# Moving two groups of buffers in SBUF: the operands of two large products of an attention and softplus feed-forward kernel

## The chip, the cores and the metric

The kernel runs on one core of a Trainium2 chip. The metric is the device time of one execution in microseconds, here the median of three executions. TensorE (PE, with its weight loads shown apart as PEld), VectorE (DVE), ScalarE (ACT), GpSimd (POOL) and the DMA queue of SyncE (SP) work side by side and are tied by semaphores.

## What is computed

```python
# q, k, v: (8, 8, 576, 64); w_in: (512, 2048); w_out: (2048, 512); all float32
scores = scale * q_chunk @ k_chunk.T          # chunks of 64 positions
attn = exp(scores - max) / (sum + 1e-9)
x = (attn @ v_chunk) as (4608, 512)
h = x @ w_in
g = maximum(h, 0) + log1p(exp(-abs(h)))       # softplus
out = g @ w_out                               # (4608, 512)
```

## The kernel before

The 4608 rows of x are taken in nine groups (`m`) of 512, and the 2048 inner columns in sixteen chunks (`fc`) of 128. For each of these 144 blocks there is a first product (`gemm1`, matmuls at line 567), a softplus chain on ACT and DVE (`u` at line 578, `g_hi` at 582, `g_lo` at 586) and a second product (`gemm2`, matmuls at line 600). The order on PE is first product of block n, second product of block n - 1, first product of block n + 1, and so on. Between them stand short bursts of 64-wide matmuls (lines 449 and 530) that make the attention of later rows; lines 342 to 390 make the attention of the first rows.

Every float32 operand is split into a high and a low part (type fp32r, 4 bytes an element), and each product is the sum of three: low times high, high times low, high times high. A matmul loads one operand into PE (LDWEIGHTS, 128 columns, 512 bytes of each partition) and streams the other past it (512 columns, 2048 bytes of each partition).

- First product, a block has 12 matmuls: four slices `c` of 128 inner rows, three terms each. Loaded: a slice of the input weights (`wi_hi`, `wi_lo`, or `wib` for the second half of the chunks). Streamed: x, as eight runs of 64 elements (256 bytes) that stand 1024 bytes apart; slice `c` begins `c` times 256 bytes into the tile.
- Second product, a block has 12 matmuls: four tiles of 128 rows, three terms each. Loaded: 128 columns of `g_lo` or `g_hi`. Streamed: one row of output weights of 512 consecutive elements (`wo_hi`, `wo_lo`, `wo_end`, or a `late` buffer).

One load belongs to each matmul and runs while the matmul before it streams; so the last matmul of a first product streams x while the first `g_lo` is loaded, and the last of a second product streams output weights while the first `wi_lo` is loaded.

```python
# gemm1, line 567: out, loaded, streamed
nc.tensor.matmul(ph, wt[:, c, fs], x[:, ts_, c, :], ...)
# gemm2, line 600
nc.tensor.matmul(pos[w["m"]][t], gg[:, ts_], wt, ...)
```

The order of all engines comes from a planner (class `Plan`) with fixed costs; it is settled before the kernel runs and knows nothing of addresses. Addresses come from the tile pools: each pool is laid behind the one before (`later`, `late`, `const`, `xpool`, `ld`, `att`, `sp`), and inside a pool the tiles stand in the order in which they were first asked for, each rounded up to 32 bytes.

Of the kernel before, what the change touches and what calls it, by code (L numbers as in the profile page):

```python
# [11 lines left out]
F32 = mybir.dt.float32  # L12
F32R = mybir.dt.float32r
I32 = mybir.dt.int32
# [3 lines left out]
BF16 = mybir.dt.bfloat16  # L18
# [129 lines left out]
def chunked_attention_softplus_ffn(  # L148
# [12 lines left out]
    P = 128  # L161
# [14 lines left out]
    UW = 512  # L176
    RAW_BUFS = 3
# [2 lines left out]
    FILL = 0.8  # L180
    LATE = 15
    STAGED = 15

    later = ctx.enter_context(tc.tile_pool(name="later", bufs=2))
    late = ctx.enter_context(tc.tile_pool(name="late", bufs=LATE))
    const = ctx.enter_context(tc.tile_pool(name="const", bufs=1))
    xpool = ctx.enter_context(tc.tile_pool(name="xpool", bufs=4))
    ld = ctx.enter_context(tc.tile_pool(name="ld", bufs=1))
    att = ctx.enter_context(tc.tile_pool(name="att", bufs=1))
    sp = ctx.enter_context(tc.tile_pool(name="sp", bufs=2))  # L190
# [5 lines left out]
    ident = const.tile([P, P], F32, name="ident")  # L196
    make_identity(nc, ident)
    half = DF // 2
    wi = [tuple(const.tile([P, KC, half], F32R, name=n) for n in ("wi_hi", "wi_lo"))]
    stage = [later.tile([P, KC * half], F32, name="wib") for _ in range(2)]  # L200
    wo_hi = const.tile([P, HALF_FC, DM], F32R, name="wo_hi")
# [16 lines left out]
    tops = [const.tile([P, UW], I32, name=f"top{j}") for j in range(TOP_BUFS)]  # L218
    for t in tops:
        nc.vector.memset(t, 0)  # L220
    live = {}

    def raw_tile():
        return ld.tile([P, 2 * UW + 2], I32, name="raw", bufs=RAW_BUFS)

# [1 line left out]
    def w_load(u, is_in, fc):  # L229
        queue = nc.gpsimd if u in LOAD_POOL else nc.sync  # L230
        raw = raw_tile()
        st = raw.bitcast(U16)[:, 1 : 4 * UW + 1]
        if is_in:
            queue.dma_start(
                st.rearrange("p (c f) -> p c f", c=KC),
                w_in_v[:, :, 4 * fc * P : 4 * (fc + 1) * P],
            )
        else:
            queue.dma_start(st, w_out_v[:, fc, :])
        live["raw", u] = raw  # L240

    def w_top(u):
        live["top", u] = tops[0]
        tops.append(tops.pop(0))
        top = live["top", u].bitcast(F16).rearrange("p (f t) -> p f t", t=2)[:, :, 1]
        src = live["raw", u].bitcast(BF16)[:, 4:].rearrange("p (f t) -> p f t", t=4)[:, :, 0]
        (nc.gpsimd.tensor_copy if u not in TOP_ACT else nc.scalar.copy)(top, src)  # L247

    def w_low(u):
        if u < STAGED:  # L250
            o = u * UW
            low = stage[o // (KC * half)][:, o % (KC * half) :][:, :UW].bitcast(I32)
        else:
            low = ld.tile([P, UW], I32, name="low", bufs=LOW_BUFS)
        src = live.pop(("raw", u)).bitcast(U32)[:, 1 : 2 * UW + 1].rearrange("p (f t) -> p f t", t=2)[:, :, 0]
        nc.scalar.activation(low, src, AF.Copy, scale=2.0**-13)
        live["low", u] = low
# [347 lines left out]
    def evacuate(w, t):  # L605
        if t % 2 == 0:
            live["out", w["m"], t // 2] = raw_tile()
        o = live["out", w["m"], t // 2][:, t % 2 * DM : (t % 2 + 1) * DM].bitcast(F32)
        (nc.vector.tensor_copy if t % 2 else nc.scalar.copy)(o, pos[w["m"]][t])
        live["o", w["m"], t] = o  # L610
# [55 lines left out]
    for u, (g, is_in, fc) in enumerate(units):  # L666
        (of_in if is_in else of_out)[fc] = u
        d = due(g) - 4
        last = [f"w_hi{u}", f"w_lo{u}"]
        users = []  # L670
        if not is_in and fc >= HALF_FC:
            for j in range(2 * (fc - HALF_FC), min(2 * (fc - HALF_FC) + 2, LATE)):
                users.append("EVVSS"[j % 5] + str(j // 5))
        pl = "POOL" if u in LO_POOL else "DVE"
        ph_ = "POOL" if u in HI_POOL else "ACT"
        staged = u < STAGED
        pool = u in LOAD_POOL
        plan.add(f"load{u}", "POOL" if pool else "SP", 0.75 if pool else 0.55, partial(w_load, u, is_in, fc),
                 urg=d - LEAD if u else LQ, kb=480,
                 take=[("raw", [f"w_top{u}", f"w_low{u}"])], after=[LOAD_AFTER])  # L680
        on_act = u in TOP_ACT
        plan.add(f"w_top{u}", "ACT" if on_act else "POOL", 0.78 if on_act else 0.77, partial(w_top, u), [f"load{u}"],
                 urg=d, take=[("top", [f"w_add{u}"])])
        plan.add(f"w_low{u}", "ACT", 0.67, partial(w_low, u), [f"load{u}"], urg=d + 0.01,
                 take=[] if staged else [("low", last)], after=[f"w_top{u}"])
        plan.add(f"w_add{u}", "DVE", 0.68, partial(w_add, u), [f"w_top{u}", f"w_low{u}"], urg=d + 1.4, port=True)
        freed = []
        if is_in and fc == HALF_FC:
            freed = [f"w_{n}{j}" for n in ("hi", "lo") for j in range(STAGED)]
        if fc:  # L690
            freed.append(f"w_hi{(of_in if is_in else of_out)[fc - 1]}")
        plan.add(last[0], ph_, 0.63 if ph_ == "POOL" else 0.61, partial(w_hi, u, is_in, fc),
                 [f"w_add{u}"] + users + freed, urg=d + 2.1)
        plan.add(last[1], pl, 1.3 if pl == "POOL" else 0.65, partial(w_lo, u, is_in, fc, pl == "POOL"),
                 [last[0]] + users, urg=d + 2.8)
# [111 lines left out]
    for w in ahead + blocks:  # L807
        g, m, fc, name = w["g"], w["m"], w["fc"], w["name"]
# [58 lines left out]
```

## Time and profile before

| | |
|---|---|
| runs | 876.37, 878.07, 879.29 us; median 878.07 us |
| the profiled execution | 878.49 us |
| its span, first to last instruction | 876.7 us |
| PE busy | 861.6 us, 98% of the span |
| PE weight loads busy | 701.5 us, 80% |
| DVE, ACT, POOL busy | 348.5, 309.4, 65.3 us |
| 16 DMA engines, share of the span | 32% |

The profile gives for each group of instructions the line, the engine, the operation, the tile that is written and those that are read. The duration of a matmul is longer than its distance to the next, since matmuls are pipelined; the distance from one start to the next tells the pace. "Granted clock" 1.00 is 2.4 GHz, 0.5 is 1.2 GHz.

### The profile page before, as it was taken

The page shows a single profiled execution, that of the slowest core. Times are in us where ns is not written, and L with a number is a line of the kernel's source. Part 1 is how long each engine was busy: PE and PEld are TensorE (multiplying, and loading weights), DVE is VectorE, ACT ScalarE, POOL GpSimd, SP SyncE. Part 2 cuts the span into 40 slices and gives each one's busy share as a digit, 9 for nine tenths or more (in the row PEclk, how much of TensorE's full clock was granted, in tenths as well). Part 3 has the DMA queues.
Part 4 walks back from the last instruction along what each step waited for, and adds up shares of the span by engine and source line. Part 5 has one row for each costly group of instructions (what it writes and reads, how often), then busy time and mean ns, then how long its engine had stood idle before and what let it go on. Part 6 is the DMA issues. An engine that isn't in the chain of part 4 may idle for free.

```text
span 876.7 us, 14820 instructions
## 1 busy us (share of the span) xinstructions
PE 861.6 (98%) x5874; PEld 701.5 (80%) x5874; DVE 348.5 (40%) x589; ACT 309.4 (35%) x483; POOL 65.3 (7%) x68
## 2 busy tenths in 40 slices
PE   8799999999999999999999999999999999999998
PEld 7677888888888888888888888888888888888886
DVE  5999964333424161525242342334241614121111
ACT  4576744332423242424242332324232424222222
POOL 0564741000000000000000000000000000000000
PEclk9999999999999999999999999999999999999999
DMA  9787753322232224231322223122322241000001
GB/s 223 186 210 218 174 146 90 67 40 49 42 96 43 49 42 104 35 63 29 71 70 56 43 47 97 39 50 42 96 42 51 41 105 33 17 29 20 1 1 48
DMA packets 209958, 63.65 MB, mean 73 GB/s; under 512 B 187105, under 2 KB 203233, under 8 KB 209889
## 3 DMA queue, kind: packets, MB, share of 16 engines
q1 hardware_dynamic: 209888, 62.71, 31.9%
q8 instruction: 46, 0.75, 0.4%
q14 instruction: 24, 0.19, 0.1%
HBM read 45.09 MB, written 9.44 MB: 62 GB/s over the span
## 4 chain that ended last, share of the span: by engine, by line
PE 89%; DMA 4%; DVE 4%; SPq 1%; issue 1%; ACT 1%; POOL 0%; DVEq 0%; POOLq 0%; ACTq 0%
PE po L600 42%; PE pa L567 41%; PE pa L530 2%; DMA raw<-in_moe_w_in_dram 2%; PE pa L449 2%; DMA raw<-in_moe_w_out_dram 1%; PE po L330 1%; DVE wib L261 1%; SPq L322 1%; DVE mx L494 0%; DVE den L510 0%; DMA q<-in_q_dram 0%; DMA x<-in_v_dram 0%; DVE g_lo L586 0%; DVE x L546 0%
## 5 line engine op out<-in xcount | busy, mean ns | idle before, releaser
L578 ACT ACTIVATE u<-pa 128x512 f32<-128x512 f32 (+1 forms) x145 | 86.2, 594 | 510.1 <-PE pa L567 505.4
L586 DVE TENSOR_TENSOR g_lo<-u,g_hi 128x512 fp32r<-128x512 f32 (+1 forms) x137 | 94.9, 693 | 295.3 <-ACT g_hi L582 295.0
L567 PE MATMUL pa<-x,wib 128*128 128x512 f32 x864 | 208.6, 390 | 0.0
L567 PEld LDWEIGHTS pa<-x,wib 128*128 128x128 f32 x864 | 161.7, 188 | 36.0 <-PE po L600 2.4
L567 PE MATMUL pa<-x,wi_hi 128*128 128x512 f32 (+1 forms) x584 | 179.3, 389 | 2.1 <-DVE x L546 2.1
L600 PE MATMUL po<-late,g_hi 128*128 128x512 f32 x540 | 172.1, 394 | 0.0
L567 PEld LDWEIGHTS pa<-x,wi_hi 128*128 128x128 f32 x584 | 109.9, 189 | 24.3 <-DVE x L546 2.3
L600 PEld LDWEIGHTS po<-late,g_hi 128*128 128x128 f32 x540 | 101.2, 187 | 24.4
L567 PE MATMUL pa<-x,wi_lo 128*128 128x512 f32 (+1 forms) x292 | 114.0, 390 | 1.3 <-POOL top L247 1.0
L600 PE MATMUL po<-wo_hi,g_lo 128*128 128x512 f32 x288 | 114.9, 399 | 0.0
L600 PE MATMUL po<-late,g_lo 128*128 128x512 f32 x288 | 114.6, 398 | 0.0
L600 PE MATMUL po<-wo_lo,g_hi 128*128 128x512 f32 x288 | 114.0, 396 | 0.0
L600 PE MATMUL po<-wo_hi,g_hi 128*128 128x512 f32 x288 | 113.5, 394 | 0.0
L582 ACT CAST g_hi<-u 128x512 fp32r<-128x512 f32 (+1 forms) x145 | 89.4, 616 | 4.4
L567 PEld LDWEIGHTS pa<-x,wi_lo 128*128 128x128 f32 x292 | 55.2, 189 | 15.7 <-PE po L600 2.9
L600 PEld LDWEIGHTS po<-wo_hi,g_lo 128*128 128x128 f32 x288 | 54.3, 188 | 13.1
L600 PEld LDWEIGHTS po<-wo_hi,g_hi 128*128 128x128 f32 x288 | 54.1, 188 | 13.2
L600 PEld LDWEIGHTS po<-late,g_lo 128*128 128x128 f32 x288 | 54.0, 187 | 13.0
L600 PEld LDWEIGHTS po<-wo_lo,g_hi 128*128 128x128 f32 x288 | 54.1, 188 | 12.8
L494 DVE TENSOR_REDUCE mx<-pa 128x8 f32<-128x512 f32 x32 | 22.0, 686 | 69.4 <-ACT x L542 69.0
L426 DVE STREAM_TRANSPOSE qe<-q 128x512 f32<-128x512 f32 x29 | 20.5, 707 | 65.5 <-DMA k<-in_k_dram 46.3
L426 DVE STREAM_TRANSPOSE ka<-k 128x512 f32<-128x512 f32 x29 | 20.6, 711 | 51.1 <-DMA k<-in_k_dram 33.8
(101 smaller groups left out, 565.9 us busy)
## 6 DMA issues: line engine op xcount, KB each, us to landing
out_dram<-raw SPq DMA_DIRECT2D x36, 256.0 KB, 2.4
raw<-in_moe_w_in_dram SPq DMA_DIRECT2D x16, 512.0 KB, 5.0
raw<-in_moe_w_out_dram SPq DMA_DIRECT2D x16, 512.0 KB, 5.0
eT<-ka SPq DMA_DIRECT2D x248, 32.0 KB, 1.9
q<-in_q_dram SPq DMA_DIRECT2D x232, 32.0 KB, 2.2
k<-in_k_dram SPq DMA_DIRECT2D x232, 32.0 KB, 2.1
q<-in_v_dram SPq DMA_DIRECT2D x60, 64.0 KB, 2.5
k<-in_v_dram SPq DMA_DIRECT2D x60, 64.0 KB, 2.5
```

Of the source, the lines that this page charges most:

```text
L261: nc.vector.tensor_tensor(low, low, live.pop(("top", u)), op=ALU.add)
L322: nc.sync.dma_start(dv[a * C : (a + 1) * C, :, c2, :], v[b, a * HP : (a + 1) * HP, c * C : (c + 1) * C, :].rearrange("h s d -> s h d"),)
L330: nc.tensor.matmul(dst[:, :P], ident, ident, start=True, stop=True)
L426: nc.vector.transpose(t, live.pop((n, i)))
L449: nc.tensor.matmul(pa[o, c2, col : col + C], qT[r, a * HP + hl, :], kT[r, a * HP + hl, :], start=True, stop=True,)
L494: nc.vector.tensor_reduce(mx, sc, axis=AX.X, op=ALU.max)
L530: nc.tensor.matmul(pa[o, a, col : col + C], vt[r, 4 * j + 2 * h2 + c2, :], eT[r, :, 4 * c2 + 2 * j + h2, :], start=True, stop=True,)
L567: nc.tensor.matmul(ph, wt[:, c, fs], x[:, ts_, c, :], start=(n == 0), stop=(n == 3 * KC - 1))
L578: nc.scalar.activation(w["u"], w["ph"], AF.Softplus)
L582: nc.scalar.copy(w["hi"], w["u"])
L586: (nc.gpsimd if pool else nc.vector).tensor_tensor(w["lo"], w["u"], w["hi"].bitcast(F32), op=ALU.subtract)
L600: nc.tensor.matmul(pos[w["m"]][t], gg[:, ts_], wt, start=(w["first"] and n == 0), stop=(w["last"] and n == 2),)
```

## The change

```diff
+    G_PAD = 48
+    X_PAD = 64
...
     half = DF // 2
+    sp.tile([P, G_PAD], F32, name="pad", bufs=1)
     wi = [tuple(const.tile([P, KC, half], F32R, name=n) for n in ("wi_hi", "wi_lo"))]
...
     for t in tops:
         nc.vector.memset(t, 0)
+    const.tile([P, X_PAD], F32, name="x_pad")
     live = {}
 
     def raw_tile():
-        return ld.tile([P, 2 * UW + 2], I32, name="raw", bufs=RAW_BUFS)
+        return ld.tile([P, 2 * UW + 16], I32, name="raw", bufs=RAW_BUFS)
...
-        src = live["raw", u].bitcast(BF16)[:, 4:].rearrange("p (f t) -> p f t", t=4)[:, :, 0]
+        src = live["raw", u].bitcast(BF16)[:, 4 : 4 * UW + 4].rearrange("p (f t) -> p f t", t=4)[:, :, 0]
```

A pad of 256 bytes goes behind the constants, one of 192 bytes ahead of the softplus buffers, and each of the three `raw` buffers (weights as they arrive, and output on its way out) grows from 4104 to 4160 bytes. Nobody reads or writes the pads. The last edit takes the same elements of `raw` as before. Every engine's instructions, their order and their waits are the same before and after; only addresses differ. The pads move what lies behind them:

| buffers | begin at byte, by the remainder of 512: before | after |
|---|---|---|
| `wib`, `late`, `ident`, `wi_hi`, `wi_lo`, `wo_hi`, `wo_lo`, `wo_end`, `top` | 128 | 128 |
| `x` (also the early loads in its place) | 128 | 384 |
| `raw`, three of them | 128, 160, 192 | 384, 448, 0 |
| `q`, `k`, `low`, `eT`, `qe`, `ka` | 224 | 64 |
| `u`, `g_hi`, `g_lo` | 352 | 384 |

From the tile's start and the slice follows where the operands of the two products begin, by the same remainders:

| product | loaded, before and after | streamed, before | streamed, after |
|---|---|---|---|
| first, slices `c` = 0 and 2 | 128, 128 | 128 | 384 |
| first, slices `c` = 1 and 3 | 128, 128 | 384 | 128 |
| second, all 12 | 352, 384 | 128 | 128 |

## Rows read from the trace of the kernel before

**Rows 1.** The page: busy times, and the span in 40 slices.
```profile
PE 861.6 (98%) x5874; PEld 701.5 (80%) x5874; DVE 348.5 (40%) x589; ACT 309.4 (35%) x483; POOL 65.3 (7%) x68
...
PE   8799999999999999999999999999999999999998
...
PEclk9999999999999999999999999999999999999999
```

**Rows 2.** Waits of PE, longest first in total (us, times, longest).
```profile
PE pa L567 <- DVE x L546: 2.1, 1, 2.1
...
PE pa L530 <- DMA x<-in_v_dram: 1.2, 2, 0.6
```

**Rows 3.** Two stretches, instructions of line 600 alone (busy, count, granted clock, DMA).
```profile
0.00:126.00 126.00, 42.27 (x168) 31.79 (x168) 0.99 0.81 199
126.00:872.60 746.60, 385.14 (x1560) 291.25 (x1560) 1.00 0.24 50
```

**Rows 4.** The chain that ended last, its end (start us, us, what).
```profile
859.13 2.73 PE pa L567 x12
861.86 2.79 PE po L600 x12
864.65 2.73 PE pa L567 x12
867.38 5.61 PE po L600 x24
```

**Rows 5.** Timeline of PE, one first product and six blocks later (start us, us).
```profile
502.25 0.39 PE L600 MATMUL po<-late,g_hi 128*128 128x512 f32 x1
502.48 0.39 PE L567 MATMUL pa<-x,wi_lo 128*128 128x512 f32 x1
...
503.16 0.39 PE L567 MATMUL pa<-x,wi_lo 128*128 128x512 f32 x1
...
503.84 0.39 PE L567 MATMUL pa<-x,wi_lo 128*128 128x512 f32 x1
...
504.52 0.39 PE L567 MATMUL pa<-x,wi_lo 128*128 128x512 f32 x1
...
535.60 0.39 PE L567 MATMUL pa<-x,wi_lo 128*128 128x512 f32 x1
```

**Rows 6.** Line 600 from 499.6 to 502.47 us: duration ns min/median/max; then its last alone.
```profile
L600 PE MATMUL po<-late,g_hi x8: 389/394/397, 499.9 to 502.2; 128*128 128x512 f32 x8
L600 PE MATMUL po<-late,g_lo x4: 393/395/397, 499.7 to 501.8; 128*128 128x512 f32 x4
...
L600 PE MATMUL po<-late,g_hi x1: 389/389/389, 502.2 to 502.2; 128*128 128x512 f32 x1
```

**Rows 7.** The same of line 567 in 502.47 to 505.1 us; then its last alone.
```profile
L567 PE MATMUL pa<-x,wi_hi x8: 389/389/396, 502.7 to 505.0; 128*128 128x512 f32 x8
...
L567 PE MATMUL pa<-x,wi_hi x1: 396/396/396, 505.0 to 505.0; 128*128 128x512 f32 x1
```

**Rows 8.** Groups of PE by shape, 126 to 870 us (busy us, mean ns).
```profile
L567 PE MATMUL pa<-x,wib 128*128 128x512 f32 x768 | 185.5, 390 | 0.0
...
L600 PE MATMUL po<-late,g_lo 128*128 128x512 f32 x260 | 103.5, 398 | 0.0
...
L600 PE MATMUL po<-wo_hi,g_hi 128*128 128x512 f32 x256 | 100.7, 393 | 0.0
```

**Rows 9.** Timeline of PE: 64-wide matmuls of the first attention rows.
```profile
15.29 1.09 PE L364 MATMUL po<-late 64*64 64x64 f32 x30
...
20.61 1.09 PE L364 MATMUL po<-ka,qe 64*64 64x64 f32 x30
...
24.08 0.69 PE L390 MATMUL pa<-late 64*64 64x64 f32 x32 [0.68 <-ACT late L378]
...
29.68 0.69 PE L390 MATMUL pa<-x,eT 64*64 64x64 f32 x32 [0.60 <-ACT x L378]
```

**Rows 10.** The chain between 75 and 125 us, and waits of ACT after 126 us.
```profile
78.56 3.37 DMA x<-in_v_dram
...
118.44 3.99 DMA raw<-in_moe_w_out_dram
...
ACT u L578 <- PE pa L567: 493.5, 126, 5.4
```

## The prediction, made before the changed kernel was run

> **What bounds the kernel now.** I read the page first: PE is busy for 98% of the span and its clock is full in all but a sliver [rows 1], so the reader is to look for what sets the pace of PE's own instructions. The waits of PE come next: the longest single one is 2.1 us, in the first 126 us, and for DMA it waits 1.2 us in all [rows 2]. The chain at the end of the run is PE alone, product after product, down to the last output [rows 4]. ACT, the engine behind PE in the softplus chain, waits 493.5 us for PE after 126 us [rows 10]. So after the start nothing but the spacing of matmuls counts, and a nanosecond of a matmul is a nanosecond of the run.
>
> Now the spacing. The first product takes its slices at 502.48, 503.16, 503.84 and 504.52 us [rows 5]: three matmuls in 0.68 us, 226.7 ns each. The second product is slower. Six whole blocks take 535.60 - 502.48 = 33.12 us [rows 5], 5.520 us a block; 24 matmuls at 226.7 ns would be 5.440 us. There are 80 ns over in each block, and a block has twelve loads of g: **6.7 ns for each load of g**. The end of the run, where two second products follow each other, agrees: 5.61 us for 24 matmuls is 233.8 ns each, 7.1 ns more than 226.7 [rows 4].
>
> Is it the load of g, or the streaming of output weights, that costs this? The last matmul of each product tells, since it streams one kind and loads the other. The last of a second product streams output weights while an input weight is loaded: 389 ns, like the matmuls of the first product, where its eleven neighbours have 393 to 397 [rows 6]. The last of a first product streams x while g is loaded: 396 ns, where its neighbours have 389 [rows 7]. So the price goes with the load of g, whatever is streamed. The groups over the whole run say the same, 390 ns against 393 to 398 [rows 8]. What sets a load of g apart from one of an input weight, in the table of remainders, is that it begins at 352 and not at 128.
>
> **The change part by part.** No instruction, wait or transfer is added or taken away; only addresses move.
>
> *x from 128 to 384.* Slices 0 and 2 streamed from 128 and will stream from 384; slices 1 and 3 go the other way. Half of the first product is 256 bytes apart before, and the other half after. And it costs the same either way: slice 0 (no distance) takes 0.68 us, slice 1 (256 apart) 0.68 us, slice 2 again 0.68 us [rows 5]. This part is worth nothing, in either direction.
>
> *g from 352 to 384.* The distance to the streamed operand goes from 224 to 256, and the load's own start from a remainder of 352 to one of 384. The trace has no load of 128 columns at 384. The ends: at best the load costs nothing at all and a matmul takes its 512 columns at the granted 2.4 GHz, 213.3 ns (20 ns less than now); at worst it costs as much as or more than it does at 352. The nearest row is the load at 128 beneath the very same streamed output weights, at 389 ns and so at the pace of 226.7 ns [rows 6], and 384 differs from 128 by just the 256 bytes that made no difference with x. I take 226.7 ns.
>
> The sum: 1560 matmuls of line 600 start after 126 us [rows 3], with as many loads of g, and PE waits for nobody there: 1560 x 6.7 ns = 10.4 us. The 168 before that [rows 3] could give 1.1 us, but there PE also waits, and the chain runs through transfers of v and of weights [rows 10]; those come no sooner, so I count half, 0.5 us. Together 10.9 us.
>
> *The other buffers.* `ka`, `qe`, `eT`, `q` and `k` go from 224 to 64. Both operands of the 64-wide matmuls are among them. Thirty such matmuls from `late` (128) take 1.09 us and thirty from `ka` and `qe` (224) take 1.09 us; thirty-two at line 390 take 0.69 us with `late` and 0.69 us with `eT` [rows 9]. So the bursts gain and lose nothing. DVE and ACT work on moved buffers too; what they take is covered by ACT's 493.5 us of waiting for PE [rows 10], and would show only if a chain of softplus fell behind by microseconds in each block. Transfers land at other remainders: no row tells remainders apart; I count nothing, and as ends the 1.2 us that PE waits for DMA now [rows 2], gained or doubled.
>
> 878.49 us of the profiled execution less 10.9 is 867.6 us. That execution was 0.4 us over the median of the runs, so for the median I say **867.2 us**.
>
> **The rivals.**
>
> *No change.* The price of a load of g may come from what the pads leave alone: g was written by ACT and DVE shortly before, and it lies near the end of the memory. For it: every load of g has these too, and the 64-wide loads from 224, as odd a start as 352, are no slower than those from 128 [rows 9]. Against it: those same 64-wide loads come from buffers high in memory, filled shortly before, and are not slow either; and all twelve loads of a block cost about the same, early or late in the product [rows 6]. It gives 878.1 us. [...]
>
> *The whole stall goes.* If 256 bytes is the distance at which loading does not disturb streaming, the second product would fall to 213.3 ns: 20 ns x 1560 = 31.2 us, 847 us. Against it: half of the first product stands at that distance and pays its 226.7 ns like the rest [rows 5]. What is left for it is that x is streamed in runs of 256 bytes and output weights in one of 2048. [...]
>
> *Half the price.* A load at 384 may pay part of what one at 352 pays, say 3.3 ns: 5.2 us gained, 873 us. No row has such a middle value.
>
> *Slower.* The price may grow with the distance by remainders between load and stream: nothing at 0, 6.7 ns at 224, and more at 256. In proportion it would be 7.6 ns: 0.9 ns x 1560 = 1.5 us more, 879.6 us. It shows as slower from 1.7 ns a load on (2.6 us, 880.7 us). Against it: the last matmul of a first product streams x from 384 with g loaded from 352, 32 bytes apart, and pays as much [rows 7]; and x at a distance of 256 pays nothing more [rows 5].
>
> **How the numbers follow.** A measurement of this kernel can tell about 0.3%, 2.6 us. Chances: the price of g goes and the rest stays, 78%; no change 10%; the whole stall 5%; half the price 4%; slower 3%. Faster 0.87, same 0.10, slower 0.03. Within the likeliest case the smallest gain is 1560 loads at the 5 ns that the groups of rows 8 differ by, 7.8 us (870.3 us), and the largest all 1728 at 7.1 ns, 12.3 us (865.8 us); with what transfers may do, the range is 864.5 to 870.5 us.
>
> **What would show it.** Right: six blocks in about 32.6 us; first and second product both at 226.7 ns; 389 ns for every matmul of both lines, the last of a first product too; line 567 unchanged in slices 0 and 1; bursts as before. Wrong: matmuls of line 600 still at 393 to 398 ns (no change), well under 389 (the whole stall), or over 398 (slower); or a spacing that falls while PE begins to wait for DMA or for g after 126 us.

## The result, and the profile after

The changed kernel takes 868.13 us (median of four, 867.25 to 870.22) against 877.35 us of the kernel before on the same chip (four runs): a ratio of 0.9896, 95% interval 0.9869 to 0.9922. That is 9.2 us less (6.8 to 11.5 us by the interval); 10.9 us were forecast, to 867.2 us, and 868.1 us lies in the range. The profiled execution took 867.25 us, with a span of 865.5 us.

The chain at the end of the changed kernel (start us, us, what; line 604 is the former 600, line 571 the former 567):

```profile
848.16 2.72 PE pa L571 x12
850.88 2.72 PE po L604 x12
853.60 2.72 PE pa L571 x12
856.32 5.45 PE po L604 x24
```

These answer to [rows 4]. The second product took 2.79 us and takes 2.72 us, as long as the first; the closing run of 24 fell from 5.61 to 5.45 us, 227 ns a matmul.

The timeline of PE at the seam of the two products, as in [rows 5]:

```profile
495.99 0.39 PE L571 MATMUL pa<-x,wi_lo 128*128 128x512 f32 x1
...
496.67 0.39 PE L571 MATMUL pa<-x,wi_lo 128*128 128x512 f32 x1
...
497.35 0.39 PE L571 MATMUL pa<-x,wi_lo 128*128 128x512 f32 x1
...
498.03 0.39 PE L571 MATMUL pa<-x,wi_lo 128*128 128x512 f32 x1
...
498.71 0.39 PE L604 MATMUL po<-late,g_lo 128*128 128x512 f32 x1
...
528.63 0.39 PE L571 MATMUL pa<-x,wi_lo 128*128 128x512 f32 x1
```

Slice after slice takes 0.68 us, as before, though each has changed places: slice 0 now streams from 384 and slice 1 from 128. Six blocks take 528.63 - 495.99 = 32.64 us, as forecast (33.12 us before). The second product's durations, ten of its twelve matmuls at line 604 between 492 and 495.5 us (ns min/median/max), against 389/394/397 of [rows 6]; then all twelve of the first product that begins at 495.99 us, whose last one took 396 ns before [rows 7]:

```profile
L604 PE MATMUL po<-late,g_hi x6: 389/389/389, 493.5 to 495.1; 128*128 128x512 f32 x6
L604 PE MATMUL po<-late,g_lo x4: 389/389/389, 493.3 to 495.3; 128*128 128x512 f32 x4
...
L571 PE MATMUL pa<-x,wi_hi x8: 389/389/389, 496.2 to 498.5; 128*128 128x512 f32 x8
L571 PE MATMUL pa<-x,wi_lo x4: 389/389/389, 496.0 to 498.0; 128*128 128x512 f32 x4
```

Where nothing is saved: the blocks that hold a burst. First the kernel before, then the changed one, at the same block (timeline; the DVE row is the one that empties the burst's PSUM tile, the PE row the next first product):

```profile
258.49 0.69 PE L530 MATMUL pa<-eT,q 64*64 64x64 f32 x32
...
262.77 0.68 DVE L499 TENSOR_TENSOR qe<-pa,mx 128x512 f32<-128x512 f32 x1
...
263.59 0.47 PE L567 MATMUL pa<-x,wi_lo 128*128 128x512 f32 x1
```

```profile
254.84 0.69 PE L534 MATMUL pa<-eT,q 64*64 64x64 f32 x32
...
259.12 0.68 DVE L503 TENSOR_TENSOR qe<-pa,mx 128x512 f32<-128x512 f32 x1
...
259.94 0.47 PE L571 MATMUL pa<-x,wi_lo 128*128 128x512 f32 x1
```

From the start of the burst to the next first product it is 5.10 us in both, though a second product stands between them; in twelve of the fifteen bursts after 120 us it is 5.10 to 5.11 us in both kernels. DVE ends at 263.45 and at 259.80 us, and the first product starts 0.14 us later each time: there DVE sets the start, and what the second product gains is waited out ahead of the next first product. The waits of PE after 126 us list none of this: the ends of matmuls are modelled, and the last matmul ahead of the gap, which starts at 263.20 us before, is given 0.40 us and so fills it.

### The profile page after: what moved, and what is told of

Same layout as the page of the kernel before. It is cut to its first block, busy times and chain, and to the rows that moved or that the text cites. A ratio compares the mean times of both kernels' runs of the same rounds, so it can differ in the third digit from the quotient of the medians.

```text
span 865.5 us, 14820 instructions
## 1 busy us (share of the span) xinstructions
PE 850.3 (98%) x5874; PEld 701.7 (81%) x5874; DVE 345.5 (40%) x589; ACT 309.3 (36%) x483; POOL 66.1 (8%) x68
## 4 chain that ended last, share of the span: by engine, by line
PE 89%; DVE 4%; DMA 2%; issue 1%; ACT 1%; POOL 1%; SPq 1%; DVEq 0%; POOLq 0%; ACTq 0%
PE po L604 42%; PE pa L571 42%; PE pa L534 2%; PE pa L453 2%; DMA raw<-in_moe_w_out_dram 1%; SPq L326 1%; PE po L334 1%; DMA raw<-in_moe_w_in_dram 1%; DVE den L514 1%; DVE wib L265 0%; POOL top L251 0%; DVE eT L477 0%; DVE g_lo L590 0%; DVE low L265 0%; ACT u L582 0%
## 5 line engine op out<-in xcount | busy, mean ns | idle before, releaser
L604 PE MATMUL po<-late,g_hi 128*128 128x512 f32 x540 | 169.3, 389 | 0.0
L604 PEld LDWEIGHTS po<-wo_hi,g_hi 128*128 128x128 f32 x288 | 54.3, 189 | 11.5
L604 PEld LDWEIGHTS po<-late,g_lo 128*128 128x128 f32 x288 | 54.0, 188 | 11.5
```

The costliest lines, as they stand in the source:

```text
L604: nc.tensor.matmul(pos[w["m"]][t], gg[:, ts_], wt, start=(w["first"] and n == 0), stop=(w["last"] and n == 2),)
```

## The experiments

All moves below are made with pads alone, so the instructions and their order are those of the kernel before. "Distance" is where the load starts less where the stream starts.

**Which of the moves it is.** The first runs moved u, g_hi and g_lo alone:

```diff
     half = DF // 2
+    sp.tile([P, 8], F32, name="pad", bufs=1)      # g at 384; 72: at 128; 40: at 0; 120: at 320
```

> The kernel before with u, g_hi and g_lo alone moved from 352 to 384; x, raw and all else stay. Theory A (a load pays by its own start: free at a multiple of 64 bytes, 6.7 ns elsewhere) and theory B (a load pays by its distance from the streamed operand's start, by remainders of 512: nothing at 0 and 256, 6.7 ns at 224): both expect the whole gain of the change, line 600 at 389 ns and 226.7 ns from start to start, about 868 us. If the moves of x, raw or q and k gave part of it, it stays short of that: 870 us or more.

Measured: 867.75 us against 877.43 us, ratio 0.9895 (0.9871 to 0.9919). The chain's rows read as in the changed kernel:

```profile
856.87 2.72 PE pa L568 x12
859.59 5.45 PE po L601 x24
```

So 32 bytes ahead of g give the whole gain. The counterpart moved x and left g:

```diff
+    sp.tile([P, 64], F32, name="pad", bufs=1)
...
+    const.tile([P, 64], F32, name="x_pad")
```

> x alone moved from 128 to 384; g stays at 352 (raw goes to 384, 416 and 448, q, k and their like to 480 on the way). If x matters as the change's words have it, line 567 and the last matmul of a first product get another price. By the equal slices of the trace before: no change, 877 us, line 567 at 389 ns, line 600 at 393 to 397 ns as before. One thing may shift: the first load of g of a block now runs beneath x streamed from 128, not 384.

Measured: 877.9 us against 879.05 us, ratio 0.9987 (0.9972 to 1.0002).

```profile
865.95 2.73 PE pa L569 x12
868.67 5.61 PE po L602 x24
```

To the hundredth these are the rows of before [rows 4]: x gives nothing.

**Is 256 bytes of distance needed?**

> The kernel before with u, g_hi and g_lo alone moved to 128, so that g is loaded from the same remainder from which output weights stream (distance 0). Theory A: free, 389 ns, about 868 us. What the change's words suggest (loaded and streamed operand must begin 256 bytes apart): the price stays or grows, 393 ns and more, 877 us or more. Theory B as read from input weights loaded under output weights (distance 0 at no price): about 868 us.

Measured: 868.03 us, ratio 0.9895 (0.9876 to 0.9915).

```profile
852.15 2.72 PE pa L568 x12
854.87 5.45 PE po L601 x24
```

No: with loaded and streamed operand at the same remainder it is as fast.

**The load's own start, or the distance?**

> The kernel before with u, g_hi and g_lo alone moved to 0, so the distance to the streamed operand is 384 (or 128 the other way) and each load of 512 bytes begins on a multiple of 512. Theory A: free, 389 ns, about 868 us. Theory B (in proportion to the nearer distance, 128): 3.8 ns a load, about 872 us. A third: the 13.3 ns that every matmul has over 512 columns at 2.4 GHz come from loads that begin at 128 or 384 and never at a multiple of 512; then line 600 falls below 226.7 ns, the run below 865 us.

Measured: 881.57 us, ratio 1.0045 (1.0030 to 1.0061): 0.45% slower than before, little, but clear of the noise.

```profile
868.70 2.76 PE pa L568 x12
871.46 5.60 PE po L601 x24
```

> The kernel before with u, g_hi and g_lo alone moved to 320: a multiple of 64 and not of 128, at a distance of 192. Theory A: free, 389 ns, about 868 us. Theory A with a grain of 128 bytes: the price stays, 393 to 398 ns, about 877 us. Theory B: 5.7 ns a load, about 876 us.

Measured: 872.51 us, ratio 0.9941 (0.9922 to 0.9959), in the middle.

```profile
858.68 2.72 PE pa L568 x12
861.40 5.51 PE po L601 x24
```

Theory A falls with these two: 0 and 320 are multiples of 64, and both pay. In proportion to the nearer distance, theory B fails too (0 costs more than it said, 320 less). To part distance from place, everything was then moved under an unmoved g:

```diff
+    later.tile([P, 120], F32, name="first_pad", bufs=1)     # all that stood at 128 to 96
...
+    sp.tile([P, 8], F32, name="pad", bufs=1)                # g back at 352
```

> Everything that stood at 128 moved to 96 (wib, late, wi, wo, x and the rest), g left at 352, its dear place: both products now have distances of 0 and 256 as in the changed kernel, but no load begins where it was free so far. Theory D (distance): all matmuls at 389 ns, 226.7 ns apart, about 868 us. Theory O (own start): loads of g stay dear (877 us), and loads of input weights at 96 may become so too (885 us and more).

Measured: 869.34 us against 879.05 us, ratio 0.9898 (0.9872 to 0.9925).

```profile
855.82 2.72 PE pa L569 x12
858.54 5.45 PE po L602 x24
```

g is loaded from 352, where it cost 6.7 ns in the kernel before, and costs nothing, because the streams now start at 96. **The distance decides, not the load's own start.**

> The kernel before with g alone moved to 256, a distance of 128 from the streamed output weights, the mirror of g at 0. Theory D with a price that depends on the distance taken either way round: like g at 0, about 5.5 ns a load and some more in the first product, about 881 us. If the direction counts (load ahead of or behind the stream), something else. Theory O: starts on multiples of 256 are dear: about 881 us too.

Measured: 881.81 us against 879.05 us, ratio 1.0029 (1.0016 to 1.0041).

```profile
868.13 2.76 PE pa L568 x12
870.89 5.60 PE po L601 x24
```

The rows are those of g at 0: distances of 128 and of 384 cost the same, and the medians from one start to the next agree at each of the 24 places of a block to 1 ns. With 0 and 256 alike free, what counts is the distance by remainders of **256**. By 256 the two are one distance, so this run says nothing on a mirror.

> The changed kernel with wi_hi and wi_lo at 160 and wo_hi, wo_lo and wo_end at 192; wib and late stay at 128, x and g at 384. So in the first eight chunks the loads of the first product begin at 160 (x streams from 384 or 128: distance 224 or 32) and those of the second at 384 with streams from 192 (distance 192). Theory D (the distance decides: free at 0 and 256, about 2.5 ns at 192, 6.7 ns at 224): matmuls with wi_hi and wi_lo pay about 4 to 7 ns, those with wo_hi and wo_lo about 2.5 ns, those with wib and late nothing: 72 blocks x 12 x (5 + 2.5) ns = 6.5 us, about 874.5 us. Theory O (the load's own start decides: free at 128 and 384): wi_hi and wi_lo pay, wo_hi and wo_lo do not: about 872 us.

```diff
+    const.tile([P, 8], F32, name="wi_pad")        # wi_hi, wi_lo: 128 to 160
...
+    const.tile([P, 8], F32, name="wo_pad")        # wo_hi, wo_lo, wo_end: 128 to 192
...
-    X_PAD = 64
+    X_PAD = 48
```

Measured: 876.8 us against 879.05 us, ratio 0.9977 (0.9966 to 0.9988); by the two ratios some 7 us of the changed kernel's gain are lost, near what theory D says. With the intervals it could be 4 to 10 us, so the time alone hardly tells theory O (some 4 us) from theory D. The chain does, since by theory O the second product would pay nothing. The chain, first in chunks with `wi_hi`, `wi_lo` and `wo_hi`, `wo_lo`, then in chunks with `wib` and `late`:

```profile
324.43 2.80 PE pa L573 x12
327.23 2.75 PE po L606 x12
...
855.75 2.72 PE pa L573 x12
858.48 2.72 PE po L606 x12
```

The first product, never dear before, pays 2.80 us as soon as its own load stands 32 from its stream (160 under 128, or under 384, which is the same by 256). The second pays 2.75 us with g at 384 and streams from 192, as it did with g at 320 and streams from 128: the same distance of 192, the same price, another place. So it has nothing to do with g being fresh, or high in memory.

**The other distances** (g alone again, `sp` pads of 88, 96 and 112 elements; one run each).

> g alone at 192: distance 64 from the streamed output weights. If the price repeats every 256 bytes of distance and is the same either way round (ahead or behind), it is that of 192: 2.5 ns a load, line 600 of before at 388 to 394 ns. If it grows from 32 (6.7 ns) to 128 it lies above 6.7 ns. If it repeats every 64 bytes it is that of 128: 5.5 ns and a slower start of the first product.

```profile
866.37 2.75 PE pa L568 x12
869.12 5.61 PE po L601 x24
```

> g alone at 224: distance 96. If the price is that of 32 wherever the distance is an odd multiple of 32, 6.7 ns; if it is the mirror of 160, the same as the run with g at 288.

```profile
865.76 2.73 PE pa L568 x12
868.50 5.63 PE po L601 x24
```

> g alone at 288: distance 160, the mirror of 96. The same price as g at 224 if only the size of the distance counts; 6.7 ns if every odd multiple of 32 costs that.

```profile
869.46 2.77 PE pa L568 x12
872.23 5.61 PE po L601 x24
```

With g at 192, 224 and 288 the single times are 880.24, 879.66 and 883.35 us, against 878.63 us. All expectations of a mirror or of a fixed price for odd multiples of 32 miss. A distance of 64 comes out near that of 128, but a price that repeats every 64 bytes is excluded by 0 and by the cheap 192. A block without a burst, first plus second product, in one trace for each distance (the sum of their median times from start to start, after 126 us):

| distance by 256 | 0 | 64 | 96 | 128 | 160 | 192 | 224 |
|---|---|---|---|---|---|---|---|
| block, us | 5.44 | 5.55 | 5.54 | 5.55 | 5.57 | 5.47 | 5.52 |

(32 was measured in the first product alone: 2.80 us against 2.72.) Only 0 is free. The side counts: 192 is cheap, 64 is not. And the price does not end with the loads that cause it: with g at 0 the first product, its operands untouched, takes 2.76 us. From start to start its first seven matmuls take 224 to 236 ns, the next four 227 ns, as in the kernel before. Its durations between 868.5 and 871.3 us there, where the kernel before has 389 for all but the last [rows 7]:

```profile
L568 PE MATMUL pa<-x,wib x12: 387/391/397, 868.5 to 871.1; 128*128 128x512 f32 x12
```


**What is left above the stream.** In the kernel before the granted clock is 0.50 from 34.9 to 38.2 us (timeline of PE in that stretch):

```profile
35.14 0.41 PE L567 MATMUL pa<-x,wi_lo 128*128 128x256 f32 x1
...
37.06 0.63 PE L600 MATMUL po<-wo_hi,g_lo 128*128 128x512 f32 x1
37.49 0.63 PE L600 MATMUL po<-wo_lo,g_hi 128*128 128x512 f32 x1
```

Nine matmuls of 256 columns take 37.06 - 35.14 = 1.92 us there, 213.3 ns each, and the first of 512 columns takes 0.43 us to the next: 1.2 columns a nanosecond at a clock of 0.50. At 1.00 that makes an estimated 2.4 a nanosecond and 213.3 ns for 512 columns; in the traces, this is what the 2.4 GHz and the 213.3 ns of the prediction rest on. The measured 226.7 ns are 13.3 ns more than this estimate.

```diff
+                rows = C if n == 1 else P
                 nc.tensor.matmul(
-                    pos[w["m"]][t], gg[:, ts_], wt,
+                    pos[w["m"]][t][:rows], gg[:, ts_][:, :rows], wt,
```

> The changed kernel, but the middle term of each tile in the second product (g_hi times the low weights) loads 64 columns in place of 128 and makes 64 output rows of its 128; the other 64 rows lack that term. Every matmul of the two products is 226.7 ns apart, 13.3 ns more than 512 columns at 2.4 GHz. If these 13.3 ns come with the bytes loaded, the matmul ahead of the smaller load (that with g_lo) drops by half of it, to about 220 ns; four of twelve, 26.7 ns a block, about 3.8 us in all. If they are a fixed price of changing the loaded operand, it stays at 226.7 ns and 868 us.

```profile
858.80 2.73 PE pa L571 x12
861.53 5.52 PE po L605 x24
```

872.54 us in a single run, with 2.75 us for a second product. Both theories said no more than 2.72, so both forecasts miss: the edit made the product slower. But it changes two things at once, the bytes that are loaded and the output rows of the matmul, and the medians from start to start within the product range from 224 to 236 ns, as they do in the first product with g at 0. So the run does not settle whether the 13.3 ns are paid by the byte or as a fixed price; where they come from stays open.

## Why the prediction was right

- *The load of g pays, not the stream* (from the last matmul of each product, [rows 6, 7]). Right as far as the matmuls with a load of g are the ones that pay: 32 bytes under g alone give the whole gain. But the run with all else at 96 gives it too and leaves g where it was; it is the pair of load and stream that pays.
- *x is worth nothing.* Right, and shown: ratio 0.9987 with x alone. The equal slices of [rows 5] had said it.
- *A load of g falls to the pace of 226.7 ns.* Right: 2.72 us for each product, and a median of 389 ns at each of the 24 places in blocks without a burst. The ground given, that 256 bytes made no difference with x, was the right one, as g at 0 and at 256 show.
- *The term 1560 x 6.7 ns = 10.4 us* was somewhat too large, though its price a load was exact. 15 of the 130 second products that start after 126 us follow a burst, and there the next first product waits for DVE, as the two timelines show; their 180 loads, 1.2 us by that price, save 0.1 us in all in the profiled pair. I had taken it that PE waits for nobody after 126 us because the list of waits showed none. The other 115 at 80 ns make 9.2 us. The profiled pair bears this out: from the first second product after the first of these bursts (126.32 us before, 124.37 us after) to the closing two (867.22 and 856.15 us) it saves 9.1 us, and the closing two save 0.16 us. That the medians of the runs differ by 9.2 us as well is in part luck, as their interval reaches from 6.8 to 11.5 us.
- *Half of 1.1 us before 126 us* cannot be checked. In the profiled pair the first burst after 120 us begins at 122.00 us and not at 123.99 us, 2.0 us sooner, more than the loads before it could give. But the same block, the first product after the next one, begins at 134.77 us before and at 132.66, 135.74 and 131.05 us in the changed kernel and with g alone at 384 and at 128, three kernels in which no load of g is dear; so this stretch is not put down to the change. It is why this pair of spans differs by 11.2 us where the medians differ by 9.2.
- *The rivals.* "No change" fell: the price went with the addresses. A load does lengthen the matmul whose stream it runs under (235 ns from start to start against 227 for the last matmul of a first product, before and after), by an amount that depends on the distance of the two. "The whole stall" fell: at no distance did a product go below 226.7 ns a matmul, so the 213.3 ns behind its 847 us, an estimate by the rows at a clock of 0.50, were reached in no product at full clock. "Slower" had the right mechanism in it, distance, and the wrong curve. The first of my two arguments against it was false: x from 384 with g from 352 is 32 bytes behind, which by 256 is the same distance, 224, as 352 from 128, and so it had to cost the same. The likeliest case did not need that argument, but it had put the price on the start at 352, and in the run with all else at 96 that start is free. That 384 would be free came out right because its ground, that 256 bytes make no difference, holds for the distance; where a load starts is not the reason.

No run beat the changed kernel: g at 384 or 128, or all at 96, are equal within their intervals.

## What to carry to other kernels

Where matmuls stand back to back and each brings its own load, compare the start-to-start time of groups that load different tiles; if one group is slower by a few nanoseconds under the same stream (here 231 to 235 ns against 227), look at the byte addresses of what is loaded and what streams meanwhile, and pad so that they begin at the same remainder of 256. This was seen with loads of 128 columns (512 bytes of each partition) under streams of 512 columns, in type fp32r; the 64-wide matmuls of this kernel showed no such price (thirty in 1.09 us from 128 and from 224 [rows 9]). Here it is the next matmul's load that runs under this matmul's stream (in the kernel before, the last matmul of a second product and the load of `wi_lo` for the next both start at 502.25 us), so the last matmul of one product pairs with the first load of the other. A gain on the busiest engine was not collected in blocks where that engine waited for another (5.10 us in both kernels), though the list of waits was silent: check that a stretch with such a handover shortened too.

## What was not expected

- The distance counts by remainders of 256 bytes, and only 0 is free among the eight multiples of 32 that were tried. The dearest (160) costs about 125 ns a block, between 10 and 11 ns for each of its loads of g; the cheapest (192) some 30 ns a block.
- The dear state lasts: with g at 0, matmuls of the following first product take 387 to 397 ns, though their own operands stand well; only one of them has a load of g beneath it.
- A load of 64 columns in place of 128, with half the output rows, made its product slower, 2.75 us for 2.72.
- Why a load and a stream should meet in this way was not tried; the runs show the period of 256 and no cause of it.
